# A linear-attention and MLP-mixer kernel: a new hand-written issue order

## The chip, the cores and the metric

The kernel runs on one core of one Trainium2 chip. The metric is the device time of one launch in microseconds (us). TensorE is called PE, VectorE DVE, ScalarE ACT, GpSimd POOL and SyncE SP. SP and ACT also issue the transfers between HBM and SBUF.

## The reference

Two stages follow each other, for B = 4 batches, H = 8 heads, S = 768 tokens and D = 48.

```python
for t in range(S):                       # attention, per batch and head
    state = alpha[t][:, None] * state + outer(k[t], v[t])
    y[t]  = q[t] @ state
x = y as (B, 768, 384)
h  = relu(x.T @ w_tok1) @ w_tok2         # token mixing, 768 -> 256 -> 768
u  = x + h.T
out = u + relu(u @ w_ch1) @ w_ch2        # channel mixing, 384 -> 1536 -> 384
```

Inputs and weights are float32; the kernel's matmuls take bf16.

## The kernel before

**Blocks.** Each batch's 768 tokens are cut into three blocks of 256, so there are 12 attention blocks, numbered 0 to 11; block n belongs to batch n // 3. A block loads four tiles, `at` (alpha), `kt`, `qt` and `vt`, of 384 KB each. Block n's steps are: logarithm (`ln`, or `P`, `ln1`, `lnP`, `r1` from block 3 on), cumulative sum by matmul (`cumw`/`cum`), exponentials (`E`, `Et`, `IE`), scaling of the keys (`kk`, `kl`, with `k0a`) and of the queries (`qq`, `ql`, with `q0r`), a cast of the values (`vb`), transposes on PE (`trk`, `trq`) and their copies out of PSUM (`evk`, `evq`), the score matmuls `G0_`, `G1_` with masks `mask0_`, `mask1_`, the state matmul `K` with its updates (`sa`, `sm`, `s0_`), swapped halves of the values (`vs0_`, `vs1_`), and the outputs: matmuls `ia`, `ib`, `y0_`, `y1_` and copies `x0_`, `x1_`. Two `x` tiles come from each block, six from a batch.

**Mixer.** A batch's mixer runs `t1` (needs the six `x` and `wt1`), `ht` (ReLU), `t2` (needs both halves of `wt2`: pieces wt20 and wt21), `u` (addition), transposes `up` and copies `ut` (batches 0 and 1; a DMA transpose `ux` later), then 24 groups `c1` of three matmuls with ReLUs `rt`, then `c2` with additions `o` and stores `st`. Weights come in pieces of 384 KB: wt10, wt11, wt20, wt21, wc10 to wc15, wc20 to wc25. Each is loaded by `ldw_` and cast to bf16 by `cw_`. The very last output tile is cut in two parts, `h0` of 320 columns and `h1` of 64.

**What sets the order.** `build` (L117) makes a list of operations; a string, `ORDER` (L375), then gives all 946 of them in one sequence, each with a letter for its engine: t PE, s ACT, v DVE, g POOL, y SP. `BUFS` gives the buffer number of each value at its first use. `Plan.run` (L81) reads both, and the last loop of the kernel (L858 to L862) emits the instructions so. There is no other scheduler; an engine runs its own letters in that sequence. `GATES`, with which one transfer could be made to wait for another, is empty. Loads sit in a pool of 20 buffers of class `in`. Fillers `f1_`, `f3_` are one or three matmuls of zeros that keep PE busy in the first 25 us.

[...]

**Completion counters.** The built program gives every DMA one of eight completion semaphores in turn, in the program's sequence; from the ninth on, a DMA's issue waits until the previous DMA on its semaphore has landed, besides waiting for its buffer. A wait on an issue stands in the instruction stream of the issuing engine. In the kernel before, 84 of the 105 DMAs are issued by SP, which has nothing else to do, and 21 by ACT: two of these ahead of the first `c1`.

Of the kernel before, what the change touches and what calls it, by code (L numbers as in the profile page):

```python
# [385 lines left out]
cum4t cw_wt21s t2_0_0t t2_0_1t IE4s s0_3v sa1_3v u_0_0v t2_0_2t kk4g ldw_wc15y trq3t u_0_1v u_0_2v t2_0_3t t2_0_5t
kl4g E4s evq3s up_0_0t t2_0_4t u_0_3v cw_wc10s u_0_5v u_0_4v up_0_1t ut_0_1s ut_0_0v ld_vt4y G1_3t G0_3t up_0_2t ib3t
mask0_3v mask1_3v trk4t ldw_wc14y c1_0_0_0t c1_0_1_0t cw_wc11g ut_0_2s c1_0_2_0t c1_0_3_1t r14s cw_wc13s ldw_wc21y
c1_0_7_1t evk4s y1_3t y0_3t rt_0_1_0v q0r4v ka4v qq4v ql4g x0_3s x1_3v rt_0_0_0v rt_0_2_0v P5g cw_wc15g c1_0_7_0t
c1_0_6_1t rt_0_7_0s rt_0_7_1s cw_wc12s rt_0_3_1s c1_0_0_1t ld_qt5y c1_0_6_0t trq4t c1_0_2_1t c1_0_4_1t ld_kt5y  # L390
ldw_wc22y sm1_3g cw_wc14g vb4g lnP5s c1_0_10_1t evq4s ldw_wc20s rt_0_0_1s rt_0_6_0v rt_0_6_1v ld_vt5s rt_0_2_1s
c1_0_11_1t c1_0_11_0t rt_0_10_1v cum5t rt_0_11_1v G0_4t G1_4t kb4s IE5s rt_0_4_1v cw_wc21g kc4g ln15s E5s c1_0_10_0t
c1_0_3_0t r15s rt_0_10_0s c1_0_9_1t vs1_4g ldw_wc23y mask0_4v rt_0_9_1s rt_0_11_0s mask1_4v ldw_wc24y c1_0_8_0t
c1_0_4_0t c1_0_8_1t ia4t q0r5v vs0_4s y0_4t rt_0_8_0s rt_0_4_0s c1_0_1_1t c1_0_5_0t K4t c1_0_9_0t ldw_wc25s rt_0_5_0s
qq5v rt_0_8_1s x0_4s rt_0_9_0s cw_wc22s rt_0_3_0v rt_0_1_1v trq5t c1_0_5_1t ld_at6y k0a5g sa0_4v cw_wc20v kk5v sm0_4v
vb5v sa1_4v c2_0_5_0t c2_0_2_0t trk5t c2_0_1_0t c2_0_1_1t evq5s ib4t kc5g rt_0_5_1s cw_wc24g c2_0_2_1t c2_0_5_1t evk5v
sm1_4v P6g G0_5t ld_kt6s G1_5t cw_wc25g vs0_5s cw_wc23s y1_4t x1_4s c2_0_2_2t c2_0_1_2t ld_at7y mask0_5v t1_1_1_0t
ln16s r16s lnP6s c2_0_5_2t ia5t y0_5t c2_0_5_3t mask1_5v ld_qt6y K5t P7g sa0_5v ln17s x0_5s t1_1_1_1t vs1_5g sm0_5v
t1_1_1_2t t1_1_1_3t cum6t ld_kt7y ld_qt7y t1_1_1_4t k0a6v t1_1_0_0t lnP7s IE6s E6s o_0_5v q0r6v c2_0_1_3t ib5t y1_5t
t1_1_0_1t t1_1_0_2t cum7t ld_vt6y t1_1_0_3t x1_5s t1_1_0_4t k0a7g t1_1_1_5t kk6g t1_1_0_5t ht_1_0v E7s IE7s o_0_1v  # L400
ld_at8y ht_1_1s ld_at10s c2_0_0_0t c2_0_4_0t vb6s r17s ld_vt7y t2_1_0t t2_1_2t c2_0_3_0t t2_1_3t c2_0_4_1t ka6g u_1_0v
u_1_3v t2_1_1t kk7v u_1_1v c2_0_3_1t t2_1_4t st_0_1y vb7s t2_1_5t ln110s c2_0_0_1t c2_0_4_2t up_1_0t u_1_2v u_1_5v
up_1_1t c2_0_4_3t ld_at9y dk6y u_1_4v ld_vt8s ld_kt8s ut_1_0v c2_0_3_2t c2_0_3_3t c2_0_0_2t up_1_2t q0r7g c2_0_0_3t
ut_1_1v ln18s r18s o_0_4v ut_1_2s c1_1_10_0t c1_1_5_0t c2_0_2_3t st_0_5y ld_qt8y qq7v c1_1_0_1t o_0_0v c1_1_2_1t
rt_1_5_0v kb6s c1_1_8_1t o_0_3v rt_1_0_1v vs1_6g kc6s vs0_7g P8g vs0_6g P9g qq6g vs1_7s c1_1_1_1t q0r8g rt_1_10_0v K6t
rt_1_2_1s r110s rt_1_1_1s lnP8s c1_1_1_0t c1_1_7_0t ka7s dk7y ld_kt9y c1_1_9_0t c1_1_9_1t s0_6v lnP9s vb8s rt_1_8_1v
rt_1_1_0v sa1_6v rt_1_9_0s c1_1_4_1t rt_1_9_1s ln19s rt_1_7_0v r19s dq6y c1_1_3_1t ld_qt9y kc7s c1_1_10_1t cum8t
o_0_2v c1_1_11_0t c1_1_3_0t c1_1_7_1t E8s ld_qt10s rt_1_10_1v IE8s c1_1_2_0t rt_1_3_1v kb7g rt_1_4_1v P10g k0a8g
sm1_6g k0a9g K7t c1_1_6_1t rt_1_3_0s rt_1_7_1v rt_1_11_0s rt_1_2_0s sa0_7v sm0_7v st_0_4y c1_1_11_1t c1_1_0_0t
rt_1_6_1s cum9t pq6s c1_1_5_1t rt_1_11_1v dq7y rt_1_0_0v sa1_7v c1_1_4_0t G1_6t G0_6t c2_1_4_0t qq8g mask0_6v  # L410
# [482 lines left out]
```

## Time and profile before

| quantity | value |
|---|---|
| time, median of three runs | 165.13 us (165.07 to 166.51) |
| span of the profiled execution | 163.8 us, 4061 instructions |
| own time of the profiled execution | not listed apart from the three runs, whose fastest is 165.07 us, 1.3 us over the span |
| PE busy | 154.4 us (94%), 1598 matmuls |
| DVE, ACT, POOL busy | 110.7 (68%), 101.8 (62%), 75.6 us (46%) |
| DMA | 34.46 MB, mean 210 GB/s; queue q1 (SP's) 66.2%, q10 (ACT's) 13.1% of the 16 DMA engines' span |
| mean granted PE clock | 0.990 |

The table of stages (windows) gives, for each stretch of the span, the busy time of each engine with its count of instructions in brackets, the granted PE clock, the busy share of the DMA engines and GB/s. The chain lists what released what, back from the end, in order of time: start, duration, engine and line. The waits list who waited for whom in total us, number of times and the longest. In the timeline a letter q behind an engine (SPq, ACTq) marks its sequencer, here the issue of a DMA; a matmul's modelled duration includes its way through the array, so back-to-back ones overlap.

### The profile page before, as it was taken

Reading aid. Unit: us, or ns where it says so; the run is one execution under the profiler, and the core shown is the slowest. Engines: PE = TensorE matmul, PEld = TensorE weight load, DVE = VectorE, ACT = ScalarE, POOL = GpSimd, SP = SyncE. Lnnn points to the kernel's source line nnn. Section 1 sums busy time; section 2 is a strip of 40 time slices with the busy share of each in tenths; the row PEclk is TensorE's granted clock in tenths of the full one; section 3 lists DMA queues with packets and bytes.
Section 4 is the critical chain, followed back from the end, with each engine's and each line's share of the span. In section 5 each row is a group of like instructions: output and inputs, shape, how many; then the busy total and the mean of one; then the engine's idle time right before and its main releaser. Section 6 shows DMA issues by size and latency. Waiting matters only on the chain.

```text
span 163.8 us, 4061 instructions
## 1 busy us (share of the span) xinstructions
PE 154.4 (94%) x1598; PEld 98.4 (60%) x1598; DVE 110.7 (68%) x197; ACT 101.8 (62%) x188; POOL 75.6 (46%) x94
## 2 busy tenths in 40 slices
...
GB/s 129 323 319 268 267 343 340 348 341 331 326 372 338 298 299 209 283 310 156 229 254 204 224 127 240 137 216 255 11 48 100 48 71 134 83 100 13 111 71 142
DMA packets 76322, 34.46 MB, mean 210 GB/s; under 512 B 68112, under 2 KB 76304, under 8 KB 76304
## 3 DMA queue, kind: packets, MB, share of 16 engines
q1 hardware_dynamic: 64704, 27.73, 66.2%
q10 hardware_dynamic: 11600, 6.49, 13.1%
...
## 4 chain that ended last, share of the span: by engine, by line
PE 57%; DMA 11%; POOL 9%; DVE 6%; ACT 6%; SPq 5%; issue 3%; ACTq 0%; POOLq 0%
PE ps L834 22%; PE ps L829 21%; DMA in<-in_v_dram 6%; PE ps L604 5%; SPq L545 4%; PE ps L810 4%; DMA in<-in_q_dram 4%; POOL pkk L653 3%; PE ps L805 2%; DMA in<-in_alpha_dram 2%; POOL vb L698 2%; DVE pkk L653 1%; PE ps L821 1%; DVE rt L802 1%; POOL in L645 1%
## 5 line engine op out<-in xcount | busy, mean ns | idle before, releaser
L834 PE MATMUL ps<-wc,rt 128*128 128x384 bf16 (+2 forms) x300 | 54.7, 320 | 0.0
L829 PE MATMUL ps<-ut,wc 128*128 128x384 bf16 x288 | 51.7, 326 | 0.2
L800 ACT ACTIVATE rt<-ps 128x384 bf16<-128x384 f32 x55 | 25.3, 494 | 25.4 <-PE ps L829 23.8
L834 PEld LDWEIGHTS <-rt 128*128 128x128 bf16 x300 | 27.6, 98 | 16.6
L829 PEld LDWEIGHTS <-wc 128*128 128x128 bf16 x288 | 27.1, 98 | 17.3 <-issue 0.7
L802 DVE TENSOR_SCALAR rt<-ps 128x384 bf16<-128x384 f32 x41 | 21.6, 552 | 13.8 <-PE ps L829 13.6
L720 DVE TENSOR_TENSOR gtm<-ps,mk 128x1024 bf16<-128x1024 f32 x24 | 28.3, 1219 | 2.7 <-PE ps L604 2.5
L653 POOL TENSOR_TENSOR pkk<-in,IE 128x384 bf16<-128x384 f32 (+1 forms) x12 | 14.3, 1206 | 9.3 <-DVE pkq L653 5.7
L838 DVE TENSOR_TENSOR o<-ps,u 128x384 f32<-128x384 f32 (+2 forms) x25 | 13.3, 536 | 6.1 <-PE ps L834 6.0
L814 DVE TENSOR_TENSOR u<-ps,x 128x384 bf16<-128x384 f32 x24 | 12.3, 553 | 4.1 <-PE ps L810 4.1
L653 POOL TENSOR_TENSOR pkq<-in,E 128x384 bf16<-128x384 f32 (+1 forms) x8 | 11.2, 1410 | 5.8 <-ACT tpk L697 2.9
L697 ACT CAST x<-ps 128x384 bf16<-128x384 f32 x19 | 9.0, 481 | 7.6 <-PE ps L604 7.6
L697 ACT CAST vb<-in 64x384 bf16<-64x384 f32 (+1 forms) x18 | 11.8, 657 | 2.6 <-POOL vb L698 1.4
L698 POOL CAST vb<-in 64x384 bf16<-64x384 f32 (+1 forms) x17 | 9.5, 559 | 8.0 <-DMA in<-in_v_dram 3.7
L805 PE MATMUL ps<-x,wt 128*128 128x384 bf16 x48 | 11.4, 326 | 0.3 <-ACT x L697 0.3
L810 PE MATMUL ps<-ht,wt 128*128 128x384 bf16 x48 | 10.1, 326 | 0.7 <-ACT wt L697 0.7
L589 POOL TENSOR_TENSOR in<-in 128x384 f32<-128x384 f32 x9 | 9.0, 999 | 3.2 <-DMA in<-in_alpha_dram 2.2
L653 DVE TENSOR_TENSOR pkq<-in,E 128x384 bf16<-128x384 f32 (+1 forms) x9 | 6.0, 689 | 6.3 <-ACT E L637 4.0
L645 POOL TENSOR_TENSOR in<-in,in 128x384 f32<-128x384 f32 x7 | 7.0, 1002 | 5.7 <-DVE in L649 3.0
L604 PE MATMUL ps<-tpq,tpk 48*64 48x128 bf16 (+1 forms) x288 | 8.5, 221 | 1.1 <-DVE ss L762 0.6
L768 DVE TENSOR_TENSOR tmp<-ps,ss 128x384 f32<-128x384 f32 x12 | 6.7, 555 | 4.1 <-POOL ss L771 2.3
L604 PEld LDWEIGHTS <-gtm 128*128 128x128 bf16 x192 | 7.6, 96 | 2.2 <-issue 0.6
...
## 6 DMA issues: line engine op xcount, KB each, us to landing
in<-in_alpha_dram SPq DMA_DIRECT2D x11, 384.0 KB, 5.9
in<-in_q_dram SPq DMA_DIRECT2D x10, 384.0 KB, 5.5
in<-in_moe_w_ch_dram SPq DMA_DIRECT2D x10, 384.0 KB, 7.4
in<-in_k_dram SPq DMA_DIRECT2D x9, 384.0 KB, 5.3
in<-in_v_dram SPq DMA_DIRECT2D x9, 384.0 KB, 5.3
...
in<-in_moe_w_tok_dram SPq DMA_DIRECT2D x3, 384.0 KB, 5.5
```

Source lines behind the costliest of these rows:

```text
L604: return self.pe.matmul(out, lhsT=lhsT, rhs=rhs, start=start, stop=stop, skip_group_check=True)
L653: self.shared(self.eng[e].tensor_tensor(self.t(dst)[:, c : c + z, :, 0:D], self.t(src)[:, :, c : c + z, :].rearrange("p h s d -> p s h d") ...
L697: return self.act.copy(d, s)
L698: return self.shared(self.eng[e].tensor_copy(d, s))
L720: self.nc.vector.tensor_tensor(self.t(gtm)[:, hf, :, :], self.pair(gp).rearrange("p a (j t) -> p (a j) t", t=128), bass.AP(tensor=m.tensor ...
L800: self.act.activation(d, s, AF.Relu)
L802: self.nc.vector.tensor_scalar_max(d, s, 0.0)
L805: self.pe.matmul(self.bank(bank)[:, 0:HD], lhsT=self.wt1[:, kc, m * 128 : m * 128 + 128], rhs=self.t(x), start=(kc == 0), stop=(kc == NS - 1))
L810: self.pe.matmul(self.bank(bank)[:, 0:HD], lhsT=self.wt2[:, kc, i * 128 : i * 128 + 128], rhs=self.t(hts[kc]), start=(kc == 0), stop=(kc = ...
L829: self.pe.matmul(self.bank(bank)[:, 0:HD], lhsT=self.wc1[:, kc, mc * 128 : mc * 128 + 128], rhs=self.t(ut)[:, 3 * half : 3 * half + 3, kc, ...
L834: self.pe.matmul(self.bank(bank)[:, 0 : cz - ca], lhsT=self.t(rts[mc][0])[:, i * 128 : i * 128 + 128], rhs=self.wc2[:, mc, ca:cz], start=( ...
L838: self.nc.vector.tensor_tensor(self.t(o)[:, ca:cz], self.bank(bank)[:, 0 : cz - ca], self.t(u)[:, i % 3, ca:cz], ALU.add)
```

## The change

`ORDER` and `BUFS` are new; no other line differs. The same 946 operations are issued, each once, in another sequence, some by another engine, into other buffers. Counts by letter:

| | PE | ACT compute | DVE | POOL | SP DMAs | ACT DMAs |
|---|---|---|---|---|---|---|
| before | 393 | 187 | 179 | 82 | 84 | 21 |
| after | 393 | 190 | 193 | 65 | 62 | 43 |

Ahead of the first `c1` the letters are: DMAs by ACT 19 (before 2), DMAs by SP 17 (29), operations on POOL 14 (23), on ACT 36 (45), on DVE 34 (35), on PE 68 (74). The six PE operations that move behind the first `c1` are K3, trq3, G1_3, G0_3, ib3 and trk4.

The cut diff, up to the first `t1` and at the end:

```diff
 ORDER = """
-f3_trk0t f1_trq0t f3_trq0t f3_cumw1t f3_cumw0t ld_at0y ln0s ld_at1y ln1s ld_qt0y ld_kt0y ld_vt0y cumw0t E0s ql0v
-ld_at2y f1_K0t f3_K0t cumw1t qq0v trq0t ld_kt1y ld_vt1y IE0s IE1s evq0v ld_qt1y Et0s vb0s kk0g E1s ld_at3y kl0g trk0t
-ln2s Et1s evk0s K0t kk1g kl1g s0_0v cumw2t vb1s vs0_0s Et2s E2s IE2s ld_qt2y vs1_0g qq1v ql1v G0_0t sa1_0t ln13s
-f1_trq1t sm1_0v f3_trq1t G1_0t K1t P3g ld_kt2y ld_vt2y lnP3s trk1t trq1t sa0_1t evk1s evq1s ld_kt3y qq2g mask0_0v
-mask1_0v ldw_wt10y ld_vt3y sm0_1v y0_0t cum3t x0_0s ib0t sa1_1t ld_at4y ld_qt3y ql2v trq2t sm1_1v kl2v E3s IE3s kk2g
-vs0_1g ldw_wt11s y1_0t evq2v G0_1t ia1t kk3g f1_G11t ldw_wt20y ldw_wt21y mask0_1v k0a3g x1_0s G1_1t ld_kt4y vb2s trk2t
...
-st_3_1y o_3_5v o_3_4v c2_3_3_3t c2_3_0h0_1t st_3_5y st_3_4y o_3_0h1v st_3_0h1y o_3_3v c2_3_0h0_2t c2_3_0h0_3t o_3_0h0v
-st_3_0h0y st_3_3s
+f1_K0t f3_K0t f3_trk0t f1_trq0t f3_trq0t ld_at0y ld_at1y f3_cumw0t f3_cumw1t ld_qt0s ln0s cumw0t ld_kt0s ln1s cumw1t
+ld_vt0s ld_qt1y E0s IE0s E1s ld_at2y ld_kt1s ld_kt2s Et1s ql0v qq0v IE1s trq0t evq0s Et0s ln2s ld_vt1s kl0v kk0v trk0t
+ld_qt2s vb0v K0t ld_vt2y evk0v G1_0t f1_trq1t s0_0v qq1g ql1g ib0t ldw_wt10y ld_at3y mask1_0v sa1_0t sm1_0v G0_0t
+f3_trq1t vs0_0s kk1v trq1t evq1s ldw_wt11s ldw_wt20s ld_kt3s ldw_wt21s kl1v cumw2t IE2s ld_at4s Et2s mask0_0v vs1_0v
+kk2g kl2g trk1t y0_0t evk1v E2s y1_0t f1_G11t G1_1t mask1_1v vb1s x0_0s ldw_wc10s K1t ldw_wc13s qq2v sa0_1t sm0_1v
+x1_0s ld_vt3s ia1t ldw_wc11s vs1_1s vs0_1s G0_1t ld_qt3y mask0_1v sa1_1t sm1_1v trk2t ql2g vb2g trq2t K2t vs0_2g
+sa0_2t vs1_2g ldw_wc14y y0_1t f3_G12t evk2v evq2s G0_2t cw_wt10g ldw_wc15s x0_1s sm0_2v ld_at5y G1_2t mask0_2v ib1t
+ln13s ia2t cw_wt11s t1_0_0_0t y1_1t t1_0_1_0t t1_0_0_1t t1_0_0_2t ib2t x1_1s y0_2t t1_0_1_1t t1_0_1_2t t1_0_0_3t
...
+c2_3_2_3t o_3_2v c2_3_5_1t c2_3_5_2t st_3_2y c2_3_5_3t o_3_5v st_3_5y c2_3_0h0_2t c2_3_0h0_3t o_3_0h0v st_3_0h0s
+c2_3_0h1_0t c2_3_0h1_1t c2_3_0h1_2t c2_3_0h1_3t o_3_0h1v st_3_0h1s
```

Read engine by engine, SP's list now begins at0, at1, qt1, at2, vt2, wt10, at3, qt3, wc14, at5, kt4, wc12, qt4, and ACT's stream is the following, with the landings and operations that the built program makes its DMA issues (in brackets) wait for:

| ACT, in its own order | the issue waits for |
|---|---|
| [qt0] ln0 [kt0] ln1 [vt0] E0 IE0 E1 | nothing |
| [kt1] [kt2] Et1 IE1 evq0 Et0 ln2 | kt1: qt0 landed, ln1; kt2: qt1 landed |
| [vt1] [qt2] vs0_0 evq1 | vt1: vt0 landed; qt2: wt10 landed, qq0 |
| [wt11] [wt20] [kt3] [wt21] IE2 | at3 landed; kt2 landed; qt3 landed; wc14 landed |
| [at4] Et2 E2 vb1 x0_0 | vt1 and kt1 landed, kl1 |
| [wc10] [wc13] x1_0 | at5 landed; qt2 landed |
| [vt3] [wc11] vs1_1 vs0_1 evq2 | kt4 landed; wt11 landed |
| [wc15] x0_1 ln13 cw_wt11 x1_1 lnP3 x1_2 IE3 ht_0_0 | wt20 landed, ql1 |

On SP, qt3 waits for kt0's landing, wc14 for at2's landing and `kk0`, at5 for vt2's landing and `ln2`, kt4 for kt1's and vt0's landing, `vs1_0` and `vs0_0`, and wc12 for kt3's and wt11's landing and `cw_wt11`.

More of the change, by code (lines that the diff above doesn't have):

```diff
@@ L386 @@
[L386 to L410, printed above, removed]
@@ new lines @@
+t2_0_5t r13s E3s t2_0_4t ldw_wc22s kl3g kk3g kb3s ldw_wc23y P4g lnP4s u_0_3v up_0_1t ut_0_1s u_0_1v up_0_0t ld_vt4y
+trk3t cum4t u_0_5v u_0_4v up_0_2t cw_wc10g ldw_wc24y cw_wc13s ut_0_0v c1_0_1_0t c1_0_0_0t ka3g kc3v evk3v ld_qt5s
+ut_0_2s ln14s r14s vb3g rt_0_1_0v IE4s c1_0_7_0t c1_0_6_0t rt_0_6_0v rt_0_0_0s vs0_3s vs1_3g c1_0_1_1t rt_0_1_1s
+c1_0_6_1t cw_wc11g c1_0_2_0t q0r3v ql3v c1_0_3_1t rt_0_2_0s c1_0_7_1t K3t rt_0_6_1v rt_0_3_1v c1_0_0_1t cw_wc14s
+rt_0_7_0s qq3g trq3t c1_0_2_1t rt_0_2_1s rt_0_7_1s c1_0_8_1t s0_3v sa1_3v c1_0_3_0t cw_wc15g P5g evq3v G1_3t rt_0_8_1v
@@ new lines @@
+ln15s G0_3t mask1_3v c1_0_9_0t E4s rt_0_3_0s lnP5s c1_0_11_1t c1_0_8_0t rt_0_0_1s ldw_wc25s c1_0_10_1t c1_0_11_0t
+mask0_3v rt_0_11_1s cum5t ib3t y1_3t c1_0_10_0t cw_wc12s c1_0_5_1t rt_0_11_0s kk4g k0a4g kl4v c1_0_4_0t rt_0_9_0s
+ld_at6s E5s x1_3s IE5s ld_kt5y qq4v y0_3t cw_wc21v q0r4v ql4v trk4t rt_0_10_1v c1_0_4_1t rt_0_4_1v rt_0_4_0v
+rt_0_10_0s trq4t c1_0_5_0t evk4s rt_0_5_0v rt_0_5_1v cw_wc20g c2_0_4_0t c2_0_1_0t evq4s G1_4t mask1_4v rt_0_8_0s
+cw_wc22g sm1_3g ld_vt5y G0_4t mask0_4v c1_0_9_1t ld_kt6y ka4g c2_0_4_1t kc4g c2_0_1_1t x0_3s t1_1_0_0t t1_1_0_1t
@@ new lines @@
+rt_0_9_1s r15s vb4g ld_at7y cw_wc24s ia4t c2_0_2_0t c2_0_2_1t cw_wc23v c2_0_2_2t vs1_4s vs0_4v y0_4t kb4s K4t
+c2_0_1_2t q0r5v qq5v cw_wc25s trq5t c2_0_1_3t ld_qt6y ld_kt7s sa0_4v sm0_4v P6g ld_at8y x0_4s t1_1_0_2t sa1_4v
+c2_0_0_0t evq5s o_0_1v ib4t y1_4t c2_0_4_2t c2_0_4_3t ld_vt6s lnP6s cum6t x1_4s t1_1_0_3t k0a5v kk5v trk5t IE6s E6s
+o_0_4v c2_0_0_1t c2_0_0_2t evk5v G1_5t mask1_5v sm1_4g G0_5t k0a6g vb5s kk6g dk6y ld_qt8y kc5s c2_0_5_0t c2_0_5_1t
+c2_0_5_2t ia5t mask0_5v ka6g c2_0_0_3t ld_qt7y P7g t1_1_1_0t ld_at9y vs0_5s ln16s K5t r16s c2_0_5_3t sa0_5v sm0_5v
@@ new lines @@
+q0r8v qq8v vb7v rt_1_3_1s c1_1_10_0t rt_1_10_0s c1_1_4_0t lnP9s qq7g rt_1_6_0v ld_kt9s rt_1_5_0v K6t rt_1_4_0v
+c1_1_4_1t c1_1_1_1t c1_1_0_1t s0_6v kb7g sa1_6v sm1_6g vb8s rt_1_4_1s pq6s c1_1_1_0t ld_at10s ka7s c1_1_11_0t
+c1_1_8_1t vs0_7s rt_1_2_0v rt_1_1_1v rt_1_8_1s c1_1_11_1t o_0_2v c1_1_8_0t rt_1_8_0s cum9t rt_1_11_1s IE9s E9s st_0_2y
+rt_1_0_1v c1_1_9_1t c1_1_9_0t c1_1_6_1t o_0_3v rt_1_9_1s rt_1_1_0s kc7v vs1_7v K7t c1_1_2_1t k0a8v kk8v ld_qt9y dq7y
+dk8y rt_1_11_0s c1_1_7_1t sa0_7v c1_1_5_1t sm0_7v sa1_7v st_0_1y rt_1_6_1v c1_1_3_0t rt_1_3_0v G0_6t ln19s rt_1_2_1s
@@ new lines @@
+ka10s ux_2_1y c1_2_6_1t IE11s c1_2_9_1t c1_2_11_1t rt_2_6_1s x1_9v ld_qt11y mask0_10v kb10g rt_2_11_1s c1_2_1_1t
+c1_2_7_1t ux_2_0y c1_2_4_1t ld_kt11y ia10t E11s vs0_10g kc10g K10t ld_vt11y y0_10t r111s q0r11v qq11v rt_2_9_1s
+rt_2_4_1s c1_2_0_1t c1_2_11_0t st_1_0s rt_2_7_1v rt_2_11_0s st_1_4y dq11y c1_2_1_0t c1_2_2_1t rt_2_1_1s c1_2_3_0t
+sa0_10v sm0_10v rt_2_1_0v sa1_10v c1_2_5_1t t1_3_0_0t t1_3_0_1t c1_2_3_1t rt_2_2_1s c1_2_8_0t vb11s c1_2_10_1t x0_10s
+t1_3_0_2t k0a11g rt_2_8_0s rt_2_0_1s kk11v c1_2_10_0t rt_2_5_1v c1_2_4_0t c1_2_6_0t rt_2_6_0v rt_2_3_1s c1_2_0_0t
```

64 lines of the change are left out of this document (31 added, 33 removed), and 22 rows, old and new, of the table BUFS.

## The prediction

> **What bounds the kernel now.** I read the table of stages first, to see where PE is short of work, then the chain, to see what PE waited for, then the DMA issues.
>
> ```profile
> core 0: us, PE busy (x) PEld busy (x) DVE busy (x) ACT busy (x) POOL busy (x), PEclk, DMA share, GB/s
> 4.00:12.00 8.00, 6.29 (x70) 3.89 (x69) 2.37 (x4) 6.80 (x11) 1.96 (x2) 0.94 1.16 322
> 12.00:20.00 8.00, 6.77 (x93) 4.31 (x92) 5.74 (x10) 6.30 (x10) 4.45 (x5) 0.85 1.01 266
> 20.00:24.00 4.00, 3.43 (x63) 2.45 (x60) 4.00 (x6) 3.97 (x8) 3.12 (x4) 1.00 1.10 338
> 24.00:32.00 8.00, 6.94 (x97) 4.43 (x91) 6.68 (x11) 7.74 (x15) 7.57 (x10) 1.00 1.12 342
> 36.00:60.00 24.00, 23.86 (x258) 15.94 (x256) 20.36 (x34) 21.27 (x42) 12.79 (x17) 1.00 1.10 330
> 60.00:120.00 60.00, 59.67 (x680) 38.15 (x677) 47.49 (x80) 41.16 (x79) 40.33 (x42) 1.00 0.94 205
> 120.00:160.00 40.00, 40.00 (x288) 24.81 (x287) 17.62 (x33) 9.48 (x21) 0.00 (x0) 1.00 0.25 78
> ```
>
> From 36 us to 160 us PE is busy for 123.53 of 124 us at full clock: there the time is the sum of its matmuls, which the change leaves as they are. Before that PE has holes, and its matmuls are few. So the change is judged by one moment, the first `c1`, from which PE has work in store, and by how much of PE's fixed work is done by then. The chain up to it:
>
> ```profile
> 252 pieces in order of time: start us, us, what
> 0.81 3.48 DMA in<-in_alpha_dram
> ...
> 12.03 5.82 DMA in<-in_q_dram
> ...
> 28.32 0.51 ACT vb L697
> 28.84 0.51 ACT vb L697
> 29.37 0.52 ACT la L595
> 29.89 0.38 ACT ht L800
> 30.27 0.73 ACT wt L697
> 31.05 1.15 PE ps L810 x6
> ...
> 160.52 0.49 DVE o L838
> ```
>
> The first tile lands at 0.81 + 3.48 = 4.3 us, qt2 at 12.03 + 5.82 = 17.85. In the end ACT works off a queue: two value halves of block 3, a logarithm of block 4, the ReLU `ht`, then the cast of `wt2`, which releases `t2` at 31.05. The stage 4 to 36 us moves data at about 320 to 340 GB/s where the queue is full: 384 KB then take 1.2 us. That is the pace of every tile in this stage; all loads up to the sixth `x` are paid at it.
>
> **The change, part by part.**
>
> *PE work that moves behind the first `c1`.* K3, trq3, G1_3, G0_3, ib3 and trk4. The rows of the last of them:
>
> ```profile
> 35.46 0.62 PE L666 MATMUL ps<-idn,pkk 128*128 128x128 bf16 x8
> 35.92 1.30 PE L829 MATMUL ps<-ut,wc 128*128 128x384 bf16 x7
> ```
>
> trk4 holds PE for 35.92 - 35.46 = 0.46 us from start to start, and trq3 is alike (0.45); K3 0.34, the two G 0.32 each and ib3 0.17 by the same reckoning: 2.0 us. The first `c1`, now at 35.92, must therefore start at 33.9 only to break even.
>
> *Loads: 19 issued by ACT ahead of the first `c1`, before 2.* What an issue costs ACT:
>
> ```profile
> 66.17 0.52 ACT L592 ACTIVATE lf<-in 128x384 f32<-128x384 f32 x1 [1.70 <-DVE u L814]
> 66.25 0.38 ACTq L545 DMA_DIRECT2D in<-in_v_dram  x1
> 66.65 0.81 ACTq L545 DMA_DIRECT2D in<-in_k_dram  x1
> 67.56 0.52 ACT L592 ACTIVATE lf<-in 128x384 f32<-128x384 f32 x1 [0.87 <-DVE u L814]
> ```
>
> The logarithm is over at 66.69, the next starts at 67.56: it is the second issue, over at 67.46, that ACT stood still for. Elsewhere an issue is free, since the sequencer runs ahead of the engine:
>
> ```profile
> 19.12 1.31 ACT L697 COPY tpq<-ps 128x1024 bf16<-128x1024 bf16 x1
> 19.61 0.44 ACTq L561 DMA_DIRECT2D in<-in_moe_w_tok_dram  x1
> 20.28 0.49 ACT L697 CAST x<-ps 128x384 bf16<-128x384 f32 x1
> ```
>
> The load of wt11 stands in the program behind x0_0 and two exponentials, and is issued before all three. So ACT's instructions ahead of an issue go on, and those behind it are not even queued until it is done. An issue of 0.4 us is hidden; one that waits is not. [...]
>
> *Waits in these issues.* That an issue waits for an unrelated tile is in the trace already; here are a row of the waits (total us, times, longest), two of the timeline and one of the DMA issues (count, KB, us to landing):
>
> ```profile
> SPq L567 <- DMA in<-in_q_dram: 1.8, 1, 1.8
> 26.88 0.39 ACTq L545 DMA_DIRECT2D in<-in_q_dram  x1
> 35.25 0.37 SPq L567 DMA_DIRECT2D in<-in_moe_w_ch_dram  x1
> in<-in_q_dram ACTq DMA_DIRECT2D x1, 384.0 KB, 8.3
> ```
>
> wc15 is issued by SP at 35.25, when qt4 (issued 26.88, landing 8.3 us later, 35.2) lands; it shares its completion counter and nothing else. SP lost 1.8 us and nobody minded. After the change such waits stand on ACT: wt21 and with it IE2 wait for wc14's landing, wc10 for at5's, and vt3, with vs1_1, vs0_1 and evq2 behind it, for kt4's. Those three ACT operations lead to block 2's masks and the sixth `x`.
>
> When does kt4 land? SP has no compute that would slow its list: at0, at1, qt1, at2, vt2, wt10, at3, qt3, wc14, at5, kt4, each as soon as its counter allows. ACT's list competes with it. How two queues share, the DMA issues of 20 to 28 us show:
>
> ```profile
> in<-in_moe_w_tok_dram SPq DMA_DIRECT2D x2, 384.0 KB, 6.1
> in<-in_moe_w_tok_dram ACTq DMA_DIRECT2D x1, 384.0 KB, 5.9
> ```
>
> Neither queue is served first (5.9 and 6.1 us to landing), so I let them go in pairs, at 2.4 us a pair: at0/qt0, at1/kt0, qt1/vt0, at2 alone (kt1 waits for ln1), vt2/kt1, wt10/kt2, at3/vt1, qt3/qt2 (qt2 waits for wt10), wc14/wt11 (wt11 waits for at3), at5/wt20, kt4/kt3 (kt3 waits for qt3). kt4 is in the last pair of 21 loads: 4.3 + 20 x 1.2 = 28.3 us. On the way the halves of block 0 come later too: at1 lands about 7.9 as the fourth load, so ACT's E0, which stands behind ln1, runs about 8.8.
>
> *From kt4's landing to the first `c1`:*
>
> ```profile
> 24.34 2.35 DVE L720 TENSOR_TENSOR gtm<-ps,mk 128x1024 bf16<-128x1024 f32 x2
> 29.51 0.56 DVE L802 TENSOR_SCALAR ht<-ps 128x384 bf16<-128x384 f32 x1 [0.83 <-PE ps L805]
> ```
>
> Issues of vt3 and wc11 0.8; vs1_1 and vs0_1 2 x 0.51 (row at 28.32); evq2 1.31 (row at 19.12); both masks of block 2 2.35; y1_2 0.4; x1_2 0.49; last `t1` and `ht_0_1` 0.8; the six `t2` with the last `u`, `up` and `ut` 3.7, which is 35.92 - 31.05 = 4.87 less the 1.2 us of trq3, the G and ib3 that lie within. Sum 10.9. First `c1` at 28.3 + 10.9 = 39.2, which is 3.3 later than now, with 2.0 us less done: PE ends 5.3 us later.
>
> Bounds. If loads go strictly in order of issue, ACT's are all ahead and kt4, whose buffer is free only after `vs1_0`, is the 22nd, at 29.5: +6.5. If SP's early loads get well ahead of ACT's, kt4 is the 18th (its place in the program), at 24.7: +1.7. I take the pairs, since 5.9 against 6.1 us is what they imply. [...]
>
> *Token weights.* wt20 is the 18th load in these pairs. wt21 is issued once wc14 has landed (23.5), as about the 23rd load, and lands near 30, which is where its cast now starts (30.27): an earlier place in the text is no earlier landing. Its cast is not needed before 34, so it no longer gates `t2`; its 0.73 us leave the chain, and so do the two value halves and the logarithm ahead of `ht` (1.5 us). All that lies beside the hold by kt4 and is worth nothing while the hold lasts.
>
> *Other engines.* POOL's 17 operations fewer and DVE's 14 more: on DVE 34 against 35 stand ahead of the first `c1`; I cost it at nothing, as both engines wait for tiles there. After it DVE has room (47.49 of 60 us). Should that fail, PE loses some tenths, either way.
>
> *Fillers.* 17 instead of 13 matmuls of zeros ahead of the first sum; they end about 6.4 us, when at0 and its logarithm have only just come. Nothing.
>
> *Tail.* Now 320 columns are last: 0.49 us of addition, then a store. After, 64 columns are last, and the store of the 320 goes out about 0.3 us earlier, under them: -0.2.
>
> *Sum.* +5.3 - 0.2 = +5.1 us on the span of 163.8: 168.9. The median of the runs is 165.13, 1.3 above the span; I carry that over: 170.2 us.
>
> **Rivals.**
>
> 1. *Faster: the holds do not bind.* Then the loads land in the written sequence, qt2 as the 11th at 4.3 + 10 x 1.2 = 16.3 instead of 17.85 (1.5 earlier), `t2` loses the cast (0.8) and ACT the 1.5 us of blocks 3 and 4: 3.8 us earlier, less 2.0, with the tail -2.0: 163.1 us. It decides from where kt4 lands before 28.3 - 5.1 = 23.2 us. For it: POOL and DVE carry less of blocks 3 and 4 early. Against it: even the 17th load lands at 23.5, and 17 loads precede kt4 in the program.
> 2. *No change: the holds eat the gain and no more*, kt4 between 22 and 24.5: 164 to 166.5 us, about 165.1.
> 3. *Slower still.* Order of issue as above (171.4), and a hold later: qt5's issue on ACT waits for wc12's landing, wc12's on SP for `cw_wt11`, and `ut_0_2` and the ReLUs stand behind qt5. wc12 issued about 33 would land about 38 to 41, and PE has four `c1` (2.0 us) without `ut_0_2`: up to 1.5 us more, 172.9.
>
> **How the numbers follow.** The slower case, rivals of its own size included, has 0.72; its own range is 166.6 (kt4 at 24.7) to 172.9. No change 0.13, faster 0.15. By over 1% (1.65 us, about what a measurement of this kernel can tell from no change): faster 0.15, same 0.13, slower 0.72. The range takes in the no-change case and the faster one to its own time, 163.0 to 173.0; below and above it I leave about 0.1 each.
>
> **What would show it.** Right: the ACT row of IE2 (L637) starts after 20 us; ACT has idle times just before vs1_1 (L697, out vb) that end with an issue of ACTq L545 or L561 to L567, released by a DMA; the first row of PE L829 starts near 39; from there PE is busy as before. The load of kt4 lands near 28. Wrong: the first `c1` before 34; ACT issues in a row of 0.4 us each without gaps; or a late `c1` with no idle time on ACT, for then another engine did it. A later stretch with PE holes of over 1 us would mean that batch 1's blocks, not the start, decide.

## The result and the profile after

The changed kernel takes 180.94 us (median of 4 runs, 179.42 to 181.64) where the kernel before took 165.1 us: a ratio of 1.093 (95% interval 1.087 to 1.100). The profiled execution has 179.42 us and a span of 177.7 us, 13.9 us more than the 163.8 us of before; all rows below are from it, and the account of the 13.9 us holds for it alone: the median run is 1.5 us longer still. Medians are over all runs; ratios leave out runs that lie more than 1.5% above the fastest of the same kernel. The forecast was slower, by 5.1 us of span, 170.2 us and at most 173.0. The sign came true; the size did not, and the measured time lies above the top of the range.

The table of stages of the kernel after, in the same stretches as in the prediction (32 to 60 us is left out):

```profile
core 0: us, PE busy (x) PEld busy (x) DVE busy (x) ACT busy (x) POOL busy (x), PEclk, DMA share, GB/s
4.00:12.00 8.00, 6.47 (x53) 3.51 (x52) 1.97 (x4) 4.17 (x7) 0.00 (x0) 1.00 1.17 325
12.00:20.00 8.00, 6.07 (x63) 3.85 (x63) 5.74 (x9) 3.90 (x6) 1.96 (x2) 0.57 1.15 340
20.00:24.00 4.00, 1.57 (x37) 1.14 (x34) 1.92 (x2) 0.49 (x1) 0.00 (x0) 1.00 1.15 335
24.00:32.00 8.00, 5.40 (x55) 3.91 (x55) 3.40 (x5) 4.11 (x8) 4.54 (x6) 0.63 1.12 346
...
60.00:120.00 60.00, 58.81 (x687) 38.07 (x686) 51.83 (x87) 46.78 (x90) 32.19 (x31) 1.00 0.99 220
120.00:160.00 40.00, 37.02 (x312) 22.37 (x309) 22.66 (x39) 13.02 (x29) 4.42 (x5) 1.00 0.36 88
```

Look at 20 to 24 us: the transfers run as fast as before (335 against 338 GB/s), yet the engines stand for most of the time: ACT works for 0.49 of 4 us (before 3.97), PE for 1.57 (before 3.43), DVE for 1.92 (before 4.00), POOL not at all (before 3.12). So it is not that less data arrives. The last two rows hold a second loss: from 60 to 160 us PE is idle for 4.17 us, before for 0.33.

The shares of the chain by engine, from the page, and pieces of the chain in order of time (start us, us, what) show what the early engines stand for:

```profile
PE 65%; DMA 15%; ACT 5%; ACTq 5%; issue 4%; DVE 4%; POOL 0%; SPq 0%; DVEq 0%; POOLq 0%
```

```profile
6.97 6.32 DMA in<-in_v_dram
13.93 4.36 PE ps L604 x41
...
19.60 1.17 ACTq L564
...
29.45 1.49 ACTq L567
...
100.83 6.28 DMA tpk<-pkq
...
125.22 4.63 DMA tpk<-pkk
```

ACT's own DMA issues (ACTq) had 0% of the chain before; now they have 5% of it. The four longest of these pieces, three in a row from 19.60 us and one at 29.45, last 1.0 to 2.2 us, not 0.4. The two transposes at 100.83 and 125.22 belong to the second loss.

The timeline of ACT (start us, us; the bracket gives idle time before, and what ended it) shows the hold at its place:

```profile
19.60 1.17 ACTq L564 DMA_DIRECT2D in<-in_moe_w_tok_dram  x1
20.82 1.04 ACTq L545 DMA_DIRECT2D in<-in_k_dram  x1
21.89 2.23 ACTq L564 DMA_DIRECT2D in<-in_moe_w_tok_dram  x1
24.25 0.81 ACT L637 ACTIVATE IE<-ps 128x768 f32<-128x768 f32 x1 [3.76 <-DMA in<-in_moe_w_tok_dram]
24.95 3.17 ACTq L567 DMA_DIRECT2D in<-in_moe_w_ch_dram  x1
25.71 0.84 ACT L697 CAST vb<-in 128x768 bf16<-128x768 f32 x1
28.70 0.48 ACT L697 CAST x<-ps 128x384 bf16<-128x384 f32 x1 [1.77 <-PE ps L604]
```

wt20, kt3 and wt21 are issued one after the other, each for 1 to 2.2 us, and IE2 behind them starts at 24.25 (before: 15.4). `vb1` follows at 25.71, and PE's K1, which needs it, has an idle time of 4.87 us in front of it:

```profile
26.60 0.82 PE L604 MATMUL ps<-vb,pkk 64*128 64x96 bf16 x16 [4.87 <-ACT vb L697]
```

wc10's issue then takes 3.17 us and wc13's, at 28.16, 0.50; x1_0 starts when both are over. (Its bracket names a matmul, but it starts 0.04 us after the end of wc13's issue.) The first `c1` starts at 42.79 us, 6.87 later than before, with 2.0 us less of PE's work done: 8.9 of the 13.9 us are lost by then. The other 5.1 us are lost later, and the tail gives 0.1 back.

### The profile page after: what moved, and what is told of

Same layout as the page of the kernel before. It is cut to its first block, busy times and chain, and to the rows that moved or that the text cites. A ratio compares the mean times of both kernels' runs of the same rounds, so it can differ in the third digit from the quotient of the medians.

```text
span 177.7 us, 4040 instructions
## 1 busy us (share of the span) xinstructions
PE 159.9 (90%) x1598; PEld 100.5 (57%) x1598; DVE 117.4 (66%) x211; ACT 100.7 (57%) x191; POOL 62.2 (35%) x77
## 3 DMA queue, kind: packets, MB, share of 16 engines
q10 hardware_dynamic: 26032, 14.16, 28.3%
## 4 chain that ended last, share of the span: by engine, by line
PE 65%; DMA 15%; ACT 5%; ACTq 5%; issue 4%; DVE 4%; POOL 0%; SPq 0%; DVEq 0%; POOLq 0%
PE ps L829 24%; PE ps L834 20%; PE ps L604 11%; DMA in<-in_alpha_dram 6%; PE ps L810 5%; DMA in<-in_v_dram 4%; DMA tpk<-pkq 4%; PE ps L805 3%; DMA tpk<-pkk 3%; PE ps L666 2%; ACTq L564 2%; ACTq L567 1%; PE ps L821 1%; ACT tpq L697 1%; ACTq L545 1%
## 5 line engine op out<-in xcount | busy, mean ns | idle before, releaser
L834 PE MATMUL ps<-wc,rt 128*128 128x384 bf16 (+2 forms) x300 | 53.6, 320 | 0.0
L800 ACT ACTIVATE rt<-ps 128x384 bf16<-128x384 f32 x62 | 28.1, 499 | 27.7 <-PE ps L829 22.1
L802 DVE TENSOR_SCALAR rt<-ps 128x384 bf16<-128x384 f32 x34 | 17.6, 550 | 11.0 <-PE ps L829 11.0
L838 DVE TENSOR_TENSOR o<-ps,u 128x384 f32<-128x384 f32 (+2 forms) x25 | 13.2, 536 | 13.6 <-PE ps L834 12.5
L653 POOL TENSOR_TENSOR pkk<-in,IE 128x384 bf16<-128x384 f32 (+1 forms) x9 | 12.2, 1361 | 13.1 <-ACT IE L637 9.2
L604 PE MATMUL ps<-vb,pkk 64*128 64x96 bf16 (+1 forms) x76 | 5.5, 241 | 8.5 <-ACT vb L697 4.9
L697 ACT CAST x<-ps 128x384 bf16<-128x384 f32 x16 | 7.7, 479 | 7.5 <-PE ps L604 7.4
L604 PE MATMUL ps<-zs 128*128 128x512 bf16 x25 | 9.5, 531 | 1.1 <-DVE zs L507 1.1
L771 POOL TENSOR_TENSOR ss<-tmp,E 128x384 bf16<-128x384 f32 x8 | 6.7, 833 | 9.6 <-DVE vb L698 5.2
L604 PEld LDWEIGHTS <-pkk 64*128 64x128 bf16 (+1 forms) x76 | 4.2, 115 | 10.1 <-issue 8.2
L604 PEld LDWEIGHTS <-tpk 48*64 48x64 bf16 (+1 forms) x288 | 6.4, 105 | 5.5 <-issue 4.3
```

What stands on the lines that cost most here:

```text
L604: return self.pe.matmul(out, lhsT=lhsT, rhs=rhs, start=start, stop=stop, skip_group_check=True)
L653: self.shared(self.eng[e].tensor_tensor(self.t(dst)[:, c : c + z, :, 0:D], self.t(src)[:, :, c : c + z, :].rearrange("p h s d -> p s h d") ...
L697: return self.act.copy(d, s)
L800: self.act.activation(d, s, AF.Relu)
L802: self.nc.vector.tensor_scalar_max(d, s, 0.0)
L834: self.pe.matmul(self.bank(bank)[:, 0 : cz - ca], lhsT=self.t(rts[mc][0])[:, i * 128 : i * 128 + 128], rhs=self.wc2[:, mc, ca:cz], start=( ...
```

## The experiments

Each run is preceded by what was expected of it; the letter of a theory holds within that text alone. First the start, then the later loss, then the parts alone.

### The start: are loads on ACT the cause at all?

The kernel before, in its own order, with 18 of its early loads given to ACT:

```diff
-... ld_qt0y ld_kt0y ld_vt0y ... ld_kt1y ld_vt1y ... ldw_wt20y ldw_wt21y ... ldw_wc10y ...
+... ld_qt0s ld_kt0s ld_vt0s ... ld_kt1s ld_vt1s ... ldw_wt20s ldw_wt21s ... ldw_wc10s ...
```

> The kernel before, with the 18 loads that the change newly gives to ACT ahead of the first c1 issued by ACT, at their old places in the sequence; nothing else. Theory A: the old order is hurt as well, first c1 at 39 us or later instead of 35.9, time 168 us or more. Theory B: the time stays within 1% of 165.1 us.

171.68 us, ratio 1.039 (1.035 to 1.044). The first `c1` of this run:

```profile
41.99 0.82 PE L829 MATMUL ps<-ut,wc 128*128 128x384 bf16 x4
```

It is 6.07 us later than the 35.92 of before, and the span is 6.0 us longer (169.8): the whole cost is in the start, and nothing was changed but the engine that issues these loads.

The other way round: the changed kernel with all 30 of its ACT loads on SP (its 13 stores on ACT stay).

```diff
-... ld_qt0s ln0s ... ld_kt0s ln1s ... ldw_wt20s ld_kt3s ldw_wt21s ...
+... ld_qt0y ln0s ... ld_kt0y ln1s ... ldw_wt20y ld_kt3y ldw_wt21y ...
```

> The changed order with all 30 of its ACT-issued loads issued by SP instead, the 13 ACT-issued stores left. Theory A (the issues hold ACT's stream: in the changed kernel they last 16.3 us in all between 9 and 32 us): the first c1 comes near 35 us instead of 42.8, and the time falls by about 8 us, to 173; PE runs at full clock through 12 to 32 us. Theory B (the new sequence itself, with its other engines and later tiles, is what is slow): the first c1 stays at 41 us or later, and the time at 178 us or more. Theory C (the loads merely land in a worse sequence, whoever issues them): no gain on ACT, but batch 0's twelve tiles land by about 18 us; time between 173 and 178.

171.99 us (169.06 to 172.3), against 165.38 us of the kernel before on the same chip. The first `c1`:

```profile
33.07 0.81 PE L829 MATMUL ps<-ut,wc 128*128 128x384 bf16 x4
```

That is 9.7 us earlier than with the loads on ACT, and 2.85 us earlier than the kernel before. Less the 2.0 us of work that the order puts behind it, the new order, with its own engines for the computing, is worth 0.85 us at the start. So theory A holds, and this order isn't what costs the start. PE's granted clock is 1.00 from 12 to 36 us in this run, where the changed kernel has 0.57 (12 to 20 us) and 0.63 (24 to 32 us): a part of the 9.7 us may come by way of the clock (the chain above has 4.36 us of matmuls from 13.93 us on), and no run tells how much.

### The start: late tiles, or ACT held?

Two things differ when ACT issues. Batch 0's first tiles land later (kt0 at 9.7 us, vt0 at 13.3, vt1 at 22.7 and qt2 at 25.0; before 7.9, 9.1, 13.2 and 17.9). And ACT itself stands in the issues. The next two runs part them. First, the first six ACT loads alone go to SP, so that the tiles land early again:

```diff
-ld_qt0s ... ld_kt0s ... ld_vt0s ... ld_kt1s ld_kt2s ... ld_vt1s
+ld_qt0y ... ld_kt0y ... ld_vt0y ... ld_kt1y ld_kt2y ... ld_vt1y
```

> The changed kernel (180.9 us, first c1 at 42.8) with the first six of its ACT loads (qt0, kt0, vt0, kt1, kt2, vt1) issued by SP at the same places of the order; the other 24 loads stay on ACT. Theory A (the ACT stream is held by the long issues from wt11 on, 2.2 us for wt21 and 3.2 us for wc10, and vb1, IE2 and the copies wait behind them): nothing of that goes, the first c1 stays at 41 us or later and the time at 179 us or more. Theory B (batch 0's first tiles land late, kt0 at 9.7 and vt0 at 13.3 where the kernel before has 7.9 and 9.1, because SP's later loads got ahead of them): vt0 lands by 9.5 us, the first c1 comes by 38 us and the time by 176 us.

179.54 us, ratio 1.084 (1.080 to 1.088). The tiles did land early, kt0 at 7.85 and vt0 at 9.06 us; all twelve of batch 0 had landed by 18.8 us (before 20.6), and the last token weight by 25.5 (before 30.8). IE2 started at 18.80, 5.4 us earlier than in the changed kernel. Yet the first `c1` gained 0.7 us only, as ACT was held again further on (the first row is the issues of wc10 and wc13, the second x1_0 behind them, the last `vs1_1`; x1_0 starts 0.03 us after the two issues, whatever matmul its bracket names):

```profile
24.51 0.94 ACTq L567 DMA_DIRECT2D in<-in_moe_w_ch_dram  x2
25.48 0.48 ACT L697 CAST x<-ps 128x384 bf16<-128x384 f32 x1 [3.99 <-PE ps L666]
27.73 0.73 ACTq L567 DMA_DIRECT2D in<-in_moe_w_ch_dram  x1
28.56 0.51 ACT L697 CAST vb<-in 64x384 bf16<-64x384 f32 x1 [2.60 <-DMA in<-in_alpha_dram]
```

```profile
42.11 0.81 PE L829 MATMUL ps<-ut,wc 128*128 128x384 bf16 x4
```

In this run wc10's issue shares its completion counter with kt3, which lands at 24.49, and wc11's with at4, which lands at 27.71; the issues start at 24.51 and 27.73, and x1_0 and `vs1_1` stand behind them. So here it is waits for unrelated landings that hold ACT, and early tiles alone do not help. Then the opposite: the next eleven loads go to SP and the first six stay on ACT.

```diff
-ld_qt2s ldw_wt11s ldw_wt20s ld_kt3s ldw_wt21s ld_at4s ldw_wc10s ldw_wc13s ld_vt3s ldw_wc11s ldw_wc15s
+ld_qt2y ldw_wt11y ldw_wt20y ld_kt3y ldw_wt21y ld_at4y ldw_wc10y ldw_wc13y ld_vt3y ldw_wc11y ldw_wc15y
```

> The changed kernel with the next eleven of its ACT loads (qt2, wt11, wt20, kt3, wt21, at4, wc10, wc13, vt3, wc11, wc15) issued by SP; the first six and the later thirteen stay on ACT. Theory A (ACT held by long issues): the first c1 comes by 38 us and the time by 176 us, though vt0 still lands near 13 us. Theory B (the first tiles late): first c1 at 41 us or later, 179 us or more. If each is half of it, this and the run with the first six moved both come out between 176 and 179 us.

172.42 us, ratio 1.041 (1.036 to 1.046). Two rows of ACT, without a long idle time in front, and the first `c1`:

```profile
19.16 0.81 ACT L637 ACTIVATE IE<-ps 128x768 f32<-128x768 f32 x1 [0.24 <-PE ps L604]
20.62 0.84 ACT L697 CAST vb<-in 128x768 bf16<-128x768 f32 x1
```

```profile
35.41 0.81 PE L829 MATMUL ps<-ut,wc 128*128 128x384 bf16 x4
```

kt0 still lands at 9.7 us and vt0 at 11.7, and yet the first `c1` comes 7.4 us earlier. Of the 9.7 us, the eleven loads alone account for 7.4, the six alone for 0.7, and the rest, 1.6 to 1.7, comes only when all thirty are moved. This run alone would not part the two causes, since some of the eleven land earlier as well (qt2 at 14.2 us instead of 25.0). The run before it does: there these tiles were early too, ACT was held, and the first `c1` stayed at 42.1. ACT held is the cause; late tiles are a small part.

### The start: is it the long issues themselves?

Only the two longest, wt21 (2.23 us) and wc10 (3.17 us), go to SP:

```diff
-... ldw_wt21s ... ldw_wc10s ...
+... ldw_wt21y ... ldw_wc10y ...
```

> The changed kernel (180.9 us) with only its two longest ACT issues, wt21 (2.2 us) and wc10 (3.2 us), given to SP at the same places. Theory J (each long issue holds ACT for its own time): vb1, which waits behind wt21 with its tile landed at 22.7 us, starts by 24 us, x1_0 by 26 us, the first c1 by 39.5 us, and the time is 175 to 177.5 us. Rival K (what takes time is room in a full queue: the next issue on ACT waits in their place): the issues of kt3, at4, wc13 or vt3 grow to 2 us and more, the first c1 stays at 41.5 us or later and the time at 179.5 us or more.

180.54 us, ratio 1.093 (1.090 to 1.096): no gain at all, as the rival said. The timeline of ACT:

```profile
18.17 3.41 ACTq L561 DMA_DIRECT2D in<-in_moe_w_tok_dram  x1
21.62 1.01 ACTq L564 DMA_DIRECT2D in<-in_moe_w_tok_dram  x1
22.67 1.35 ACTq L545 DMA_DIRECT2D in<-in_k_dram  x1
24.15 0.81 ACT L637 ACTIVATE IE<-ps 128x768 f32<-128x768 f32 x1 [4.66 <-issue]
26.54 3.54 ACTq L567 DMA_DIRECT2D in<-in_moe_w_ch_dram  x1
```

wt11's issue went from 0.37 to 3.41 us, wc13's from 0.50 to 3.54. The time didn't belong to an issue; it passed to the next one on ACT. In the changed kernel the DMA engines are busy throughout from 4 to 32 us (shares of 1.12 to 1.17, 325 to 346 GB/s), and one load lands per 1.2 us (19 from 5.21 us, when at0 has landed, to 28.23). ACT's fourteen issues from 9 to 32 us last 1.2 us each in the mean; that they wait for their share of the transfers, whichever they are, is an estimate from these two numbers. That they wait for room in a full queue, as rival K has it, was not shown: no row names what they wait for. Nor is the total a clean test of it: on SP, wt21 and wc10 were issued 12 and 14 us earlier (at 9.88 and 11.06 us), and vt1 and qt2 then landed 2.2 us later (at 24.8 and 27.2). What this took back of a gain wasn't parted.

### The later loss: a store ahead of ReLUs

PE's largest late hole (an idle time of 2.02 us), with the row of the ReLU on ACT that ends it, in the kernel after:

```profile
155.72 0.56 DVE L802 TENSOR_SCALAR rt<-ps 128x384 bf16<-128x384 f32 x1 [2.39 <-PE ps L829]
156.20 0.55 DVE L838 TENSOR_TENSOR o<-ps,u 128x384 f32<-128x384 f32 x1
156.78 0.34 ACTq L585 DMA_DIRECT2D out_dram<-o  x1
157.16 0.49 ACT L800 ACTIVATE rt<-ps 128x384 bf16<-128x384 f32 x1 [5.34 <-DVE o L838]
157.71 1.48 PE L829 MATMUL ps<-ut,wc 128*128 128x384 bf16 x8 [2.02 <-ACT rt L800]
```

ACT stood for 5.34 us. Its next instruction was the store st_2_1, which waits for the addition o_2_1; o_2_1 stands on DVE behind a ReLU that waited for PE (first row); and PE waits for a bank of PSUM that a ReLU behind the store would empty. The order wrote the store a few places too early. Moved, with the two next stores:

```diff
-o_2_1v st_2_1s rt_3_2_0s c1_3_10_1t st_2_5s rt_3_1_0s st_2_4s rt_3_6_1s
+o_2_1v rt_3_2_0s c1_3_10_1t rt_3_1_0s rt_3_6_1s
...
-rt_3_7_1s c2_3_4_0t
+rt_3_7_1s st_2_1s st_2_5s st_2_4s c2_3_4_0t
```

> The changed kernel with the three stores st_2_1, st_2_5 and st_2_4 moved behind rt_3_7_1 on ACT; nothing else is touched. Theory C (the store that waits for o_2_1 holds the ReLUs behind it on ACT, and TensorE waits 2.2 us for their banks at 155 us): that hole goes and the time is 178.7 us (178 to 179.3). Rival D (the banks are short there anyway, as the run with every store on SP got back what it saved in another hole): 180.5 us or more.

178.25 us, ratio 1.077 (1.073 to 1.081), 2.7 us better in the median; the two profiled executions are 1.7 us apart. PE has no idle time left there:

```profile
154.00:160.00 6.00, 6.00 (x39) 3.61 (x38) 1.95 (x4) 3.40 (x8) 0.00 (x0) 1.00 0.01 3
```

An engine other than ACT would do as well, one should think: all 13 ACT stores on SP.

```diff
-st_0_5s ... st_1_5s ... st_2_1s ... st_2_5s ... st_2_4s ...
+st_0_5y ... st_1_5y ... st_2_1y ... st_2_5y ... st_2_4y ...
```

> The changed order with its 13 ACT-issued stores issued by SP, loads left. Theory D (the store of output tile 1 of batch 2 holds ACT from 152 to 157 us, waiting for an addition on DVE, and PE loses 2.2 us there): the hole at 155.7 to 157.7 us goes and the time falls by about 2.2 us, to 178.7. Rival: the hole is due to the additions and ReLUs on DVE, and stays; time within 0.5 us of the changed kernel.

182.67 us, ratio 1.106 (1.102 to 1.111): worse. The hole at 155 us went, and this one came:

```profile
113.88 1.02 DVE L838 TENSOR_TENSOR o<-ps,u 128x384 f32<-128x384 f32 x2 [0.15 <-PE ps L834]
114.93 0.34 SPq L585 DMA_DIRECT2D out_dram<-o  x1
115.38 1.23 SPq L677 DMA_TRANSPOSE tpk<-pkk  x1
118.61 0.64 PE L604 MATMUL ps<-tpq,tpk 48*64 48x128 bf16 x16 [2.29 <-DMA tpk<-pkk]
```

Now a store on SP (st_1_5) waits for its addition, the transpose dk10 stands behind it on SP, and the scores wait for the transpose. And the wait is dearer than its 2.3 us: PE's granted clock is 0.50 after it.

```profile
118.61:125.00 6.39, 5.57 (x32) 2.88 (x33) 1.56 (x2) 2.28 (x5) 0.50 (x1) 0.50 1.04 229
```

With all DMAs on SP, both changes together:

```diff
-ld_qt0s ... st_2_1s ...
+ld_qt0y ... st_2_1y ...
```

> The changed order with all DMAs on SP. Theories A and D together: about 171 us, the first c1 near 35 us and no hole at 155 us. If some 5 us over the kernel before remain, the sequence itself costs them (theory B in part). If SP, now with 105 DMAs in one stream, is late with stores and transposes, new holes after 100 us show it.

177.04 us in the median, but from 173.0 to 186.47, too wide to compare. The profiled execution (173.0 us) has both effects: the first `c1` at 32.97, and idle times of PE of 2.33 and 0.96 us, ended by two transposes at 108.76 and 110.21, ahead of batch 2's `c1`.

Both repairs that worked, together: loads on SP, the three stores later on ACT.

```diff
-ld_qt0s ... o_2_1v st_2_1s rt_3_2_0s ...
+ld_qt0y ... o_2_1v rt_3_2_0s ... rt_3_7_1s st_2_1s st_2_5s st_2_4s ...
```

> The changed kernel with its 30 ACT loads on SP and the three stores of batch 2 moved behind rt_3_7_1 on ACT. Theory A and C together (the start and the store's hold are separate costs): first c1 near 33 us, the hole of 2.2 us near 147 us and the slow clock behind it (four gaps, 1.7 us) gone: 168.3 us at most 169.5. Rival (the hole moves, or the clock falls anyway): 171 us or more. By either it stays above the kernel before, since the small holes from 79 to 121 us are still there.

169.58 us, ratio 1.027 (1.023 to 1.032), 0.1 us above the bound that was set. The first `c1` is at 33.05 and the place of the hole is full:

```profile
144.50:153.00 8.50, 8.50 (x55) 5.08 (x52) 3.65 (x8) 4.14 (x10) 0.00 (x0) 1.00 0.02 7
```

What is left are mainly four idle times of PE between 79 and 123 us, of 0.46, 0.63, 1.19 and 0.74 us. None of the versions that were run beats the kernel before.

### The parts alone: order, engines, the weight

The new order with the engine that each operation has in the kernel before (187 letters):

```diff
-... ld_qt0s ln0s ... qq1g ql1g ...
+... ld_qt0y ln0s ... qq1v ql1v ...
```

> The order of the changed kernel with every operation on the engine that it has in the kernel before (187 of them: loads, stores, copies, scalings, ReLUs). Theory E (the issuing engine of the loads costs the start, and the other engines of copies, ReLUs and stores cost the later holes): first c1 near 33 to 34 us as with the loads on SP, no later hole over 1 us, 163 to 166 us. Rival F (the later holes come from the order itself: transposes and stores late on their queues): first c1 near 33 to 34 us, but 4 us or more of later holes, 168 us or more.

208.18 us, ratio 1.256 (1.249 to 1.262): far worse than both kernels; rival F's time (168 us or more) is met, but not the early start that both theories expected. The first `c1` is at 40.58, though ACT issues one load only (wt11) ahead of 34 us. So a late start can come without ACT's issues; what makes it here was not looked into. After it PE waits everywhere (table of stages):

```profile
40.00:120.00 80.00, 62.06 (x615) 38.05 (x613) 49.17 (x82) 48.11 (x90) 40.55 (x45) 0.98 0.71 179
120.00:206.00 86.00, 73.00 (x664) 44.39 (x662) 40.99 (x69) 28.45 (x62) 19.30 (x22) 0.98 0.40 101
```

The reverse, the order of before with the new engines:

```diff
-... ld_qt0y ... qq1v ql1v ...
+... ld_qt0s ... qq1g ql1g ...
```

> The order of the kernel before (165 us) with every operation on the engine that it has in the changed kernel (187 of them). Theory G (order and engines were laid out for each other: an engine's stream is the order restricted to it, and the reverse mixture gave 208 us): 180 us or more, with later holes spread over all batches. Rival H (the engines of copies, scalings and ReLUs weigh little; only the loads on ACT cost, and those gave 171.7 us on this order): 170 to 174 us.

195.78 us, ratio 1.184 (1.179 to 1.188). That is theory G: order and letters are one plan, as an engine's stream is the order restricted to its letters. So no share of the 13.9 us can be given to "other engines" alone.

One part of the change alone, the second token weight right behind batch 0's tiles, on the kernel before and on SP:

```diff
-ldw_wt10y ld_vt3y ... ld_at4y ld_qt3y ... ldw_wt20y ldw_wt21y
+ldw_wt10y ldw_wt20y ldw_wt21y ld_vt3y ... ld_at4y ld_qt3y ...
```

> The kernel before (165.1 us) with one part of the change alone: the loads of both halves of the second token weight issued by SP right behind wt10, ahead of vt3, at4 and qt3; engines and all else as before. Theory L (the cast of wt20 at 30.2 us, behind its landing at 29.7 us, is what releases the second token product): the product starts up to 0.8 us earlier, ahead of 30.4 us, the first c1 by as much, and the time is 164.3 us. Rival M (what is passed pays: qt3 lands 2.4 us later, at 31 us, its scalings take 3 us on POOL as before, and the transpose trq3, which stands on TensorE ahead of the later products, comes at 34 us instead of 32.0): the product starts earlier and the first c1 1 to 2 us later, at 37 to 38 us, 166 to 167 us. In neither is it 1.5 us better than the kernel before.

167.88 us, ratio 1.015 (1.011 to 1.020), 0.9 us above the rival's range. In the profiled execution, the fastest of six (166.11 us), wt20 landed at 23.75 (before 29.71) and the product that needs it started not earlier but 1.34 us later:

```profile
27.26 0.83 ACT L697 CAST vb<-in 128x768 bf16<-128x768 f32 x1 [1.49 <-DMA in<-in_v_dram]
31.51 1.55 ACT L697 CAST wt<-in 128x768 bf16<-128x768 f32 x2
```

vt3, which was passed, landed at 27.24 instead of 25.36. Its cast stands on ACT ahead of the ReLU `ht` and of the weight's cast, so all of these came 1.3 us later. The first `c1` is at 37.08, late as the rival said, though by ACT and not by qt3. The other runs are 0.5 to 3.4 us longer than this one; no row shows why.

## Why the prediction was right and where it failed

The span grew by 13.9 us and not by 5.1. Of the 8.8 us between, two steps of the prediction missed nearly all: the hold of ACT was priced 3.6 us too low at the first `c1`, and 5.1 us of later loss stood in the sum at nothing ("from there PE is busy as before").

*The moment that decides.* Right for two thirds: 8.9 of the 13.9 us are lost by the first `c1`. Wrong that PE then runs on as before: it loses 5.1 us more. The text had named this sign itself (later holes of over 1 us), but the sum had no term for it. What it overlooked: the order also moved stores and transposes of batches 1 to 3, and a store that waits held its engine as well (ACT stood for 5.34 us ahead of 157.16). Counted from matmul to matmul, less the usual step, the holes over 1 us are 2.2 us at 155 (store, shown by moving it) and 1.1 us each at 107 and 129, where PE waits for what follows a DMA transpose (chain rows at 100.83 and 125.22). These two weren't tried. In the run with the three stores moved, whose instructions are the same up to 150 us, PE has no idle time at 107, and 1.48 us at 119 where the changed kernel has none: these smaller holes differ from execution to execution, and what makes them stays open, as do some 0.7 us in small gaps.

*Landings.* Right in time, in part by luck: kt4 lands at 28.23 (predicted 28.3, by pairs), wt21 at 30.3 (predicted about 30). But at0 landed at 5.2 us and not at 4.3, and kt4 was the 20th load to land and not the 21st, since it came ahead of kt3; the two nearly cancel. The loads of the two queues did land nearly in turn: of the first 20 landings 11 are SP's and 9 ACT's, and 14 of the 19 steps from one to the next change the queue.

*kt4's landing as the hold.* Wrong, though its time fits. vt3's issue starts at 28.73, after kt4; but the issue of wc13 just ahead of it on ACT was over only at 28.66. Without any wait for kt4 it could have come 0.07 us sooner. ACT was held by the length of its issues all along, from 19.6 us on. Holds by a landing, as the prediction had them, do occur, but elsewhere: in the run with the first six loads on SP. There vt3 is issued at 25.55 (it shares its counter with wt21, which landed at 25.53), before kt4 has landed (35.54), and the first `c1` is still at 42.11.

*The size.* This is the step that failed at the start: "Issues of vt3 and wc11 0.8". They took 0.69 and 1.49 us, and with wc13's issue, which was still going on when kt4 landed, `vs1_1` came at 31.04 and not at 29.0; the term was 2.0 us too low. From there to the first `c1` it was 11.75 us instead of 10.1. Of this, 0.7 us are a transpose and a sum of later blocks (trk3 and cum4, chain rows at 41.80 and 42.24) that the new order puts between the `up`s and that the 3.7 us of the prediction left out; PE's granted clock is 0.63 from 24 to 32 us, which fits a slower block 2, but no run tried that apart. Together 14.6 instead of 10.9 us from kt4's landing. All fourteen issues from 9 to 32 us took 16.3 us, not fourteen times 0.4. The price of 0.4 was read from rows at 19 and 66 us of a kernel in which ACT issued two early loads; between 9 and 32 us of this one, with the DMA engines busy throughout (shares of 1.12 to 1.17), only six of the fourteen were 0.5 us or shorter. SP's rows at the same place would have told it: qt3 took 2.00 and wt20 2.16 us to issue there.

*"The sequencer runs ahead of the engine".* Only past work that was ready, as far as the rows show. kt0's issue stands behind ln0 in ACT's stream, vt0's behind ln1:

```profile
5.23 0.84 ACT L598 ACTIVATE la<-in 128x768 bf16<-128x768 f32 x1 [3.15 <-DMA in<-in_alpha_dram]
5.24 0.39 ACTq L545 DMA_DIRECT2D in<-in_k_dram  x1
6.96 0.84 ACT L598 ACTIVATE la<-in 128x768 bf16<-128x768 f32 x1 [0.89 <-DMA in<-in_alpha_dram]
6.97 0.47 ACTq L545 DMA_DIRECT2D in<-in_v_dram  x1
```

Each issue starts 0.01 us after the start of the logarithm, which had waited for its tile (ACT's idle time is 3.15 and 0.89 us). In the kernel before, wt11's issue (19.61 us) overtook x0_0 and two exponentials while ACT was at a copy (19.12 to 20.43), and ACT had no idle time ahead of the three; here neither issue overtook the logarithm that waited for a landing. Nor did what stands behind an issue start during it: IE2's sum was over on PE at 20.1 us and ACT stood idle for 3.76 us, but IE2 started at 24.25, after wt21's issue was over (24.12).

*Other engines, at nothing.* It is not a term that can be had alone: either mixture of order and engines is 31 to 43 us slower than the kernel before. *Tail:* -0.1 where -0.2 was forecast. *Fillers:* no run tried them apart.

*The rivals.* The faster one needed ACT not to be held; with the loads on SP the first `c1` indeed comes 2.85 us earlier than before, but the later holes and the clock behind them (0.63 after the hole in the last batch) turn that into 172 us. The slower one (a hold by qt5) isn't there: qt5 is issued in 0.37 us at 41.28, with PE busy.
